# A fused attention and feed-forward kernel: the first batch in quarters of both weights, every engine in program order, and an ELU of relu and exp on ScalarE

## The chip, the cores and the metric

One core of a Trainium2 chip. The metric is the time of one execution in microseconds (us), measured on the device. The kernel before takes 883.1 us (median of 3 runs, 882.61 to 883.67). The experiments ran in rounds on four chips; the medians of the kernel before in them differ by 1.4 us, so differences of that size between experiments of different rounds can't be told from noise. In the profile PE is TensorE (matmuls), PEld its weight loads, DVE is VectorE, ACT is ScalarE, POOL is GpSimd, SP is SyncE; PEclk is the granted TensorE clock as a share of full speed. A float32 matmul shows as two records (passes) in these traces: the 544 matmuls of the second product are 1088 records in the page of the kernel before, and the 64 of a batch are 128. Where a line says x16, and where the text counts matmuls in a line of a trace, these are passes.

## The reference

Eight batches of eight heads. Each batch has 512 tokens and 32 state rows a head, of width 64. Tokens read the state and the state reads the tokens; the results go through a feed-forward layer with ELU. The weights arrive as float64.

```python
B, H, S, Ns, D = (8, 8, 512, 32, 64)
scores = scale * x @ state.T            # [512 x 32] a head
xread  = softmax(scores) @ state        # the tokens' result
scores2 = scale * state @ x.T           # [32 x 512] a head
sread  = softmax(scores2) @ x           # the states' result
x = concat([xread, sread], axis=2)      # -> (B * 544, 512)
h = x @ w_in                            # w_in  512 x 2048, float64
g = np.where(h > 0.0, h, np.exp(np.minimum(h, 0.0)) - 1.0)   # ELU
return g @ w_out                        # w_out 2048 x 512, float64
```

## The kernel before

The kernel never forms `xread`. For each quarter c of the hidden dimension it makes `m = state @ w_in` (the product of 32 state rows with 512 columns, per head), and then `h = a @ m`. A batch has 16 hidden tiles `fo` of 128 rows; the second product adds up 16 x 4 matmuls in four banks, as the text calls the 128x512 tiles of PSUM that the kernel's matmuls write. Where the text says that PE, DVE or ACT stands, that engine is idle, waiting for another. Float64 weights are made float32 in tiles of 128x512, 16 of `w_in` and 16 of `w_out`, by three instructions on ACT and four on DVE:

```python
def convert(dst, raw):
    words = raw.bitcast(U32).rearrange("p (j w) -> p j w", w=2)
    lo, hi = words[:, :, 0], words[:, :, 1]
    nc.scalar.activation(out=lo.bitcast(FP32), in_=lo, func=AF.Copy, scale=2.0**-29, bias=2.0**23)
    nc.scalar.activation(out=lo, in_=lo.bitcast(FP32), func=AF.Copy, bias=-(2.0**23))
    nc.scalar.activation(out=dst, in_=hi.bitcast(FP32), func=AF.Abs)
    nc.vector.tensor_scalar(out=dst, in0=dst, ...)            # clamp
    bits = dst.bitcast(U32)
    nc.vector.tensor_scalar(out=bits, in0=bits, ...)          # shift, mask
    nc.vector.scalar_tensor_tensor(out=bits, in0=hi, ...)     # sign
    nc.vector.tensor_tensor(out=bits, in0=bits, in1=lo, op=ALU.add)

def make_m(b, c):                       # m = state @ w_in, one quarter
    ...
    ps = by_state(b, "m_ps", [w_in[:, m, cols] for m in range(NP)])
    for g in range(G):
        (nc.scalar.copy, nc.vector.tensor_copy)[g % 2](out=m_t[b, c][:, g], in_=ps[:, g])

def elu(ps, g, fo):
    e = epool.tile([P, n], FP32, tag="e", name="e_sb")
    nc.scalar.activation(out=e, in_=ps, func=AF.Exp)
    nc.vector.tensor_scalar(out=e, in0=e, scalar1=1.0, scalar2=None, op0=ALU.min)
    nc.vector.scalar_tensor_tensor(out=g[fo], in0=e, scalar=-1.0, in1=ps, op0=ALU.add, op1=ALU.max)

...
for b in range(B):                      # batch 0 is the one with the weights
    g = {}
    for fo in range(FO):
        ffn1(g, b, fo)                  # h and ELU
        if b == 0:
            more(1)                     # one more conversion
        if fo % 4 == (3 if b == 0 else 1) and fo // 4 + 1 < FC:
            make_m(b, fo // 4 + 1)
    if b == 0:
        more(len(rest))                 # the 9 that are left, all of w_out
    hooks = attention(b + 1) if nxt else []
    ...                                 # second product, with the next
                                        # attention between its matmuls
```

Only PE keeps its written order here (`tc.keep_in_program_order` around each matmul and transpose). The instructions of ACT, DVE and POOL are placed by the scheduler when the program is built.

Of the kernel before, what the change touches and what calls it, by code (L numbers as in the profile page):

```python
# [25 lines left out]
def kernel(  # L26
# [23 lines left out]
    NB = S // 32  # L50
    scale = 1.0 / math.sqrt(D)
# [20 lines left out]
    rawpool = pool("raw", 7)  # L72
# [12 lines left out]
    def matmul(*args, **kw):  # L85
        tc.keep_in_program_order(nc.tensor.matmul(*args, **kw))  # L86

    def transpose(out, in_):
        tc.keep_in_program_order(nc.tensor.transpose(out, in_, ident))  # L89
# [22 lines left out]
    def load_states():  # L112
        s_v = state.rearrange("(q b) (m c) n d -> q c b n m d", q=2, c=2)
        raw = [
            rawpool.tile([P, NP, P], FP32, tag="raw", name="s_sb").rearrange(
                "p m (c d) -> p m c d", c=2
            )
            for q in range(2)
        ]
        for q in range(2):  # L120
            for b in range(B // 2):
                for c in range(2):
                    (nc.sync, nc.scalar)[q].dma_start(
                        out=raw[q][b * NS : (b + 1) * NS, :, c], in_=s_v[q, c, b]
                    )
        return raw

    def turn_states(raw):
        ps = banks([P, 2, NP, P], "k_ps")
        for q in range(2):  # L130
            for m in range(NP):
                transpose(ps[:, q, m], raw[q][:, m].rearrange("p c d -> p (c d)"))
        nc.vector.tensor_copy(
            out=kT.rearrange("p m (q s) -> p q m s", q=2), in_=ps
        )

    def load_weights(src):
        k = src.shape[-1]
        raw = rawpool.tile([P, 512], moe_w_in.dtype, tag="raw", name="raw")
        nc.sync.dma_start(out=raw.rearrange("p (j k) -> p j k", k=k), in_=src)  # L140
        return raw

    def convert(dst, raw):



        words = raw.bitcast(U32).rearrange("p (j w) -> p j w", w=2)
        lo, hi = words[:, :, 0], words[:, :, 1]

        nc.scalar.activation(  # L150
            out=lo.bitcast(FP32), in_=lo, func=AF.Copy, scale=2.0**-29, bias=2.0**23
        )
        nc.scalar.activation(out=lo, in_=lo.bitcast(FP32), func=AF.Copy, bias=-(2.0**23))


        nc.scalar.activation(out=dst, in_=hi.bitcast(FP32), func=AF.Abs)
        nc.vector.tensor_scalar(  # L157
            out=dst, in0=dst, scalar1=as_float(896 << 20),
            scalar2=as_float((1151 << 20) - 1), op0=ALU.max, op1=ALU.min,
        )  # L160

        bits = dst.bitcast(U32)
        nc.vector.tensor_scalar(  # L163
            out=bits, in0=bits, scalar1=3, scalar2=0x3FFFFFF8,
            op0=ALU.logical_shift_left, op1=ALU.bitwise_and,
        )
        nc.vector.scalar_tensor_tensor(  # L167
            out=bits, in0=hi, scalar=0xC0000000, in1=bits,
            op0=ALU.bitwise_and, op1=ALU.bitwise_or,
        )  # L170
        nc.vector.tensor_tensor(out=bits, in0=bits, in1=lo, op=ALU.add)  # L171
# [10 lines left out]
    def turn_x(b, i):  # L182

        ps = banks([P, 2, R, P], "xT_ps")
        for j in range(2):
            for r in range(R):
                m = 2 * i + j
                transpose(ps[:, j, r], x_t[b][:, r, m * P : (m + 1) * P])
        xT = xtpool.tile([P, 2, R * P], FP32, name="xT")
        for j in range(2):  # L190
            st[b, 2 * i + j] = xT[:, j]
            nc.scalar.copy(out=xT[:, j], in_=ps[:, j].rearrange("p r q -> p (r q)"))  # L192
# [18 lines left out]
    def scores(b):  # L211

        ps = by_state(b, "s_ps", [st[b, m] for m in range(NP)])
        for g in range(G):
            softmaxes(b, g, ps[:, g])

    def softmaxes(b, g, ps):

        top = small.tile([P, 1], FP32, name="top")
        total = small.tile([P, 1], FP32, name="total")  # L220
        nc.vector.reduce_max(top, ps, axis=AX_X)  # L221
        nc.vector.tensor_scalar(
# [3 lines left out]
        nc.vector.transpose(t.rearrange("p k n -> p (k n)"), ps)  # L226
        a = apool.tile([P, S], FP32, name="a_s")
        st[b, g, "a_s"] = a
        nc.scalar.activation(  # L229
            out=a, in_=ps, func=AF.Exp, scale=scale, bias=top, accum_out=total  # L230
        )

        top_t = small.tile([P, NB], FP32, name="top_t")
        total_t = small.tile([P, NB], FP32, name="total_t")
        nc.vector.reduce_max(top_t, t, axis=AX_X)  # L235
        nc.gpsimd.tensor_tensor(out=t, in0=t, in1=bc(top_t, NS), op=ALU.subtract)  # L236
        nc.scalar.activation(out=t, in_=t, func=AF.Exp, scale=scale)

        nc.vector.tensor_scalar(
            out=total, in0=total, scalar1=eps, scalar2=None, op0=ALU.add  # L240
        )
        nc.vector.reciprocal(out=total, in_=total)
        nc.vector.tensor_scalar(out=a, in0=a, scalar1=total, scalar2=None, op0=ALU.mult)

        nc.vector.reduce_sum(total_t, t, axis=AX_X)
        nc.vector.tensor_scalar(
            out=total_t, in0=total_t, scalar1=eps, scalar2=None, op0=ALU.add
        )
        nc.vector.reciprocal(out=total_t, in_=total_t)
        nc.gpsimd.tensor_tensor(out=t, in0=t, in1=bc(total_t, NS), op=ALU.mult)  # L250
        st[b, g, "t"] = t

    def turn_tokens(b, g):
        st[b, g, "aT"] = atpool.tile([P, S], FP32, name="aT")
        nc.vector.transpose(st[b, g, "aT"], st[b, g, "t"].rearrange("p k n -> p (k n)"))

    def turn_state(b):
# [6 lines left out]
        for g in range(G):  # L264
            nc.scalar.copy(out=st[b, "aT_s"][:, g], in_=ps[:, g])  # L265

    def state_read(b):
# [11 lines left out]
        for g in range(G):  # L279
            rows = slice(g * D, (g + 1) * D)  # L280
            nc.vector.tensor_copy(  # L281
# [3 lines left out]
    def make_m(b, c):  # L285
# [4 lines left out]
        for g in range(G):  # L290
            (nc.scalar.copy, nc.vector.tensor_copy)[g % 2](out=m_t[b, c][:, g], in_=ps[:, g])  # L291

    def elu(ps, g, fo):
# [3 lines left out]
        nc.scalar.activation(out=e, in_=ps, func=AF.Exp)  # L297
        nc.vector.tensor_scalar(out=e, in0=e, scalar1=1.0, scalar2=None, op0=ALU.min)  # L298
        g[fo] = gpool.tile([P, n], FP32, tag="g", name="g_sb")
        nc.vector.scalar_tensor_tensor(  # L300
# [3 lines left out]
    def ffn1(g, b, fo):  # L304
# [10 lines left out]
        elu(ps, g, fo)  # L315
# [14 lines left out]
    def ffn2(g, chunks, o_sb, hooks, every):  # L330

        ps = [ps_o.tile([P, DM], FP32, tag="o", name="o_ps") for c in chunks]
        done = 0
        for fo in range(FO):
            for c, o_ps in zip(chunks, ps):
                matmul(
                    o_ps,
# [8 lines left out]
        for c, o_ps in zip(chunks, ps):  # L346
            (nc.scalar.copy, nc.vector.tensor_copy)[c % 2](out=o_sb[c // 2][:, c % 2], in_=o_ps)  # L347

    def attention(b):

        nop = lambda: None
        steps = [lambda: turn_x(b, 0), lambda: turn_x(b, 1), lambda: scores(b), nop, nop]
# [3 lines left out]

    make_identity(nc, ident)
    raw_states = load_states()
    load_x(0, [nc.sync, nc.scalar])
    todo = [load_w_in(0, n) for n in range(NP)]  # L360
    turn_states(raw_states)
    steps = attention(0)
    for f in steps[:3]:
        f()
    for f in todo:
        f()
    todo = [load_w_in(1, n) for n in range(NP - 1)]
    make_m(0, 0)
    for f in steps[3:]:
        f()  # L370
    for f in todo:
        f()
    rest = [lambda c=c, n=n: load_w_in(c, n) for c in range(1, FC) for n in range(NP)][NP - 1 :]
    rest += [lambda fo=fo: load_w_out(fo) for fo in range(FO)]

    def more(k):
        for f in rest[:k]:
            f()()
        del rest[:k]

    for b in range(B):
        g = {}
        for fo in range(FO):
            ffn1(g, b, fo)
            if b == 0:
                more(1)
            if fo == 2 and b == 0:
                load_x(1, [nc.sync])
            if fo % 4 == (3 if b == 0 else 1) and fo // 4 + 1 < FC:
                make_m(b, fo // 4 + 1)  # L390
        if b == 0:
            more(len(rest))
        nxt = b + 1 < B
        hooks = attention(b + 1) if nxt else []
        if b + 2 < B:
            hooks += [lambda: load_x(b + 2, [nc.sync])]
        rows = out_b[b, 0:S].rearrange("(p r) c -> p r c", r=R)
        o_sb = [opool.tile([P, 2, DM], FP32, name="o_sb") for i in range(2)]
        for chunks in [[0, 1, 2], [3]] if b == 0 else [[0], [1], [2], [3]]:
            if nxt and chunks == [3]:  # L400
                hooks += [lambda: make_m(b + 1, 0)]
            ffn2(g, chunks, o_sb, hooks, 4)
            for i in range(2):
                if 2 * i + 1 in chunks:
                    nc.sync.dma_start(out=rows[:, 2 * i : 2 * i + 2], in_=o_sb[i])
# [3 lines left out]
    g = {}  # L409
    for fo in range(FO):  # L410
        ffn1_state(g, fo)
    o_sb = [opool.tile([P, 2, DM], FP32, name="o_sb")]
    for c in range(2):
        ffn2(g, [c], o_sb, [], 1)
        for i in range(P // NS):
            nc.sync.dma_start(
                out=out_b[c * (P // NS) + i, S:SB], in_=o_sb[0][i * NS : (i + 1) * NS, c]
            )
# [30 lines left out]
```

## Time and profile before

| | kernel before |
|---|---|
| time, median of 3 | 883.1 us |
| profiled run: span, mean clock | 882.8 us, 0.990 |
| PE busy | 838.0 us (95%) |
| DVE busy | 323.8 us, 658 instructions |
| ACT busy | 214.0 us, 386 instructions |
| batch 1's first product starts | 168.94 us |

PE is the bound from about 140 us on (busy for all 28.9 us from 140.0 to 168.9, and for 709.3 of the 713.9 behind them); the prediction shows the views for that. Here are the lines of PE's own timeline in batch 0 that have a wait, with the first h and the last line for their length (start, duration, what, count, and in brackets the idle time before with what ended it):

```profile
48.70 9.05 PE L86 MATMUL h_ps<-aT,m_sb 128*128 128x512 f32 x16
...
61.12 1.12 PE L86 MATMUL h_ps<-aT,m_sb 128*128 128x512 f32 x2 [2.36 <-ACT m_sb L291]
62.78 7.97 PE L86 MATMUL h_ps<-aT,m_sb 128*128 128x512 f32 x14 [0.54 <-DVE m_sb L291]
...
74.01 1.13 PE L86 MATMUL h_ps<-aT,m_sb 128*128 128x512 f32 x2 [2.24 <-ACT m_sb L291]
76.54 7.95 PE L86 MATMUL h_ps<-aT,m_sb 128*128 128x512 f32 x14 [1.41 <-DVE m_sb L291]
...
87.27 1.13 PE L86 MATMUL h_ps<-aT,m_sb 128*128 128x512 f32 x2 [1.76 <-ACT m_sb L291]
89.80 7.97 PE L86 MATMUL h_ps<-aT,m_sb 128*128 128x512 f32 x14 [1.40 <-DVE m_sb L291]
...
126.02 2.37 PE L89 MATMUL sT_ps<-ident,a_s 128*128 128x128 f32 x8 [4.68 <-ACT a_s L229]
128.18 5.07 PE L86 MATMUL o_ps<-w_out,g_sb 128*128 128x512 f32 x8
```

Between the first h at 48.70 and batch 1 at 168.94 PE stands still for 14.4 us in all (the sum of the brackets). Each group of 16 h matmuls takes about 9.1 us, though 8 of them take 3.43 at full clock (at 263.63, PEclk 1.00), so 16 should take 6.9: about 2.2 us a group are lost, 8.9 us in four groups, most of it to slow passes. In three of the groups PEclk shows them: 0.50 from 62.9 to 66.3, 0.51 from 76.5 to 80.0, 0.56 from 89.8 to 93.0. In the group at 48.70 it reads 1.00, but weight loads start 0.86 us apart until 52.2 and 0.43 from 52.9 on. The transposes at 126.02 lose 1.3 (1.04 at 101.04, PEclk 1.00), and the eight passes behind them 1.5 (5.07 for 3.60), at a clock of 0.50 from 126.0 to 131.0. So **everything that a better order of batch 0 can take out after 48.70 is about 14.4 + 8.9 + 1.3 + 1.5 = 26.1 us**.

### The profile page before, as it was taken

How to read it: one execution, taken by the hardware profiler on the slowest of the kernel's cores; microseconds unless marked ns; L12 is line 12 of the kernel's file. 1: busy time of each engine (PE TensorE's matmuls, PEld its weight loads, DVE VectorE, ACT ScalarE, POOL GpSimd, SP SyncE). 2: the span in 40 equal slices, each digit the busy share in tenths (PEclk: the TensorE clock that was granted, in tenths of full speed). 3: DMA queues.
4: the chain of work that ended last, by engine and by line, in shares of the span. 5: the costliest groups of instructions: out<-in, count | busy, mean ns of one | idle time of the engine just before them, and what ended most of it. 6: DMA issues, size and time to landing. Idle time of an engine off the chain costs nothing.

```text
span 882.8 us, 7236 instructions
## 1 busy us (share of the span) xinstructions
PE 838.0 (95%) x2824; PEld 391.5 (44%) x2824; DVE 323.8 (37%) x658; ACT 214.0 (24%) x386; POOL 35.8 (4%) x38
## 2 busy tenths in 40 slices
PE   3487979999999999999999999999999999999997
PEld 2242435444543454445444454445434544444763
DVE  2869980263105340444026301632053403500220
ACT  4757730132003210222013201321033102200110
POOL 0200010001000010001000100001000100000000
PEclk9999989999999999999999999999999999999999
DMA  8564502100300011000200030000000000000000
GB/s 256 149 177 155 184 9 48 48 1 1 71 1 25 0 36 36 25 0 1 72 24 1 1 71 25 0 1 25 0 25 0 1 25 24 1 0 25 24 1 24
DMA packets 42914, 35.07 MB, mean 40 GB/s; under 512 B 36480, under 2 KB 36480, under 8 KB 42880
## 3 DMA queue, kind: packets, MB, share of 16 engines
q1 hardware_dynamic: 39648, 33.82, 12.9%
q10 hardware_dynamic: 3232, 0.79, 0.4%
q8 instruction: 22, 0.36, 0.2%
q14 instruction: 12, 0.10, 0.0%
HBM read 25.69 MB, written 8.91 MB: 39 GB/s over the span
## 4 chain that ended last, share of the span: by engine, by line
PE 89%; DVE 6%; DMA 2%; ACT 2%; issue 1%; POOL 0%; SPq 0%; ACTq 0%
PE o_ps L86 51%; PE h_ps L86 28%; PE sr_ps L86 4%; PE m_ps L86 3%; PE xT_ps L89 1%; DMA raw<-in_moe_w_in_dram 1%; DVE w_out L167 1%; PE sT_ps L89 1%; PE s_ps L86 1%; DVE w_out L171 1%; DVE w_out L157 1%; DVE g_sb L300 0%; DVE w_out L163 0%; DVE w_in L167 0%; DMA x_sb<-in_x_dram 0%
## 5 line engine op out<-in xcount | busy, mean ns | idle before, releaser
L86 PE MATMUL o_ps<-w_out,g_sb 128*128 128x512 f32 x1088 | 478.6, 595 | 0.0
L86 PEld LDWEIGHTS o_ps<-w_out,g_sb 128*128 128x128 f32 x1088 | 204.1, 191 | 252.3 <-issue 249.3
L86 PE MATMUL h_ps<-aT,m_sb 128*128 128x512 f32 x512 | 235.3, 613 | 9.7 <-ACT m_sb L291 6.4
L86 PEld LDWEIGHTS h_ps<-aT,m_sb 128*128 128x128 f32 x512 | 97.6, 195 | 146.0 <-issue 105.0
L297 ACT ACTIVATE e_sb<-h_ps 128x512 f32<-128x512 f32 (+1 forms) x144 | 82.5, 573 | 247.7 <-PE h_ps L86 247.6
L298 DVE TENSOR_SCALAR e_sb<-e_sb 128x512 f32<-128x512 f32 (+1 forms) x144 | 59.3, 412 | 104.2 <-ACT e_sb L297 104.0
L300 DVE SCALAR_TENSOR_TENSOR g_sb<-e_sb,h_ps 128x512 f32<-128x512 f32 (+1 forms) x144 | 94.6, 657 | 4.5
L347 DVE COPY o_sb<-o_ps 128x512 f32<-128x512 f32 x17 | 11.7, 691 | 175.4 <-PE o_ps L86 175.4
L291 DVE COPY m_sb<-m_ps 128x512 f32<-128x512 f32 x32 | 22.1, 690 | 116.7 <-ACT m_sb L291 116.7
L347 ACT COPY o_sb<-o_ps 128x512 f32<-128x512 f32 x17 | 9.8, 579 | 216.0 <-PE o_ps L86 216.0
L86 PE MATMUL m_ps<-w_in,kT 64*32 64x512 f32 x512 | 39.5, 615 | 10.7 <-ACT a_s L229 7.4
L236 POOL TENSOR_TENSOR t_sb<-t_sb,top_t 128x512 f32<-128x512 f32 x16 | 16.9, 1059 | 645.0 <-DVE top_t L235 518.1
L221 DVE TENSOR_REDUCE top<-s_ps 128x1 f32<-128x512 f32 x16 | 11.0, 685 | 68.2 <-PE s_ps L86 68.2
L86 PEld LDWEIGHTS sr_ps<-aT_s,x_sb 128*128 128x128 f32 x256 | 33.0, 209 | 4.9 <-issue 3.3
L86 PE MATMUL sr_ps<-aT_s,x_sb 128*128 128x64 f32 x256 | 32.9, 292 | 1.2 <-ACT aT_s L265 1.2
L291 ACT COPY m_sb<-m_ps 128x512 f32<-128x512 f32 x32 | 18.7, 585 | 42.7 <-PE m_ps L86 42.7
L86 PE MATMUL h_ps<-xT_state,w_in 128*128 128x256 f32 x128 | 27.8, 379 | 0.0
L192 ACT COPY xT<-xT_ps 128x512 f32<-128x512 f32 x32 | 17.1, 588 | 43.6 <-PE xT_ps L89 43.6
L86 PEld LDWEIGHTS h_ps<-xT_state,w_in 128*128 128x128 f32 x128 | 24.3, 190 | 3.7 <-issue 0.5
L150 ACT ACTIVATE raw<-raw 128x512 f32<-128x512 uint32 x32 | 21.8, 680 | 12.9 <-DMA raw<-in_moe_w_in_dram 9.2
L86 PEld LDWEIGHTS m_ps<-w_in,kT 64*32 64x32 f32 x512 | 6.2, 105 | 39.4 <-issue 23.5
L281 DVE COPY xT_state<-sr_ps 64x128 f32<-64x128 f32 x16 | 4.6, 289 | 51.0 <-PE sr_ps L86 50.9
(42 smaller groups left out, 306.1 us busy)
## 6 DMA issues: line engine op xcount, KB each, us to landing
raw<-in_moe_w_in_dram SPq DMA_DIRECT2D x16, 512.0 KB, 5.0
raw<-in_moe_w_out_dram SPq DMA_DIRECT2D x16, 512.0 KB, 3.3
out_dram<-o_sb SPq DMA_DIRECT2D x16, 512.0 KB, 2.6
x_sb<-in_x_dram SPq DMA_DIRECT2D x30, 256.0 KB, 4.3
x_sb<-in_x_dram ACTq DMA_DIRECT2D x2, 256.0 KB, 4.7
out_dram<-o_sb SPq DMA_DIRECT2D x8, 64.0 KB, 1.7
s_sb<-in_state_dram SPq DMA_DIRECT2D x8, 32.0 KB, 2.1
s_sb<-in_state_dram ACTq DMA_DIRECT2D x8, 32.0 KB, 3.1
```

The costliest lines, as they stand in the source:

```text
L86: tc.keep_in_program_order(nc.tensor.matmul(*args, **kw))
L89: tc.keep_in_program_order(nc.tensor.transpose(out, in_, ident))
L150: nc.scalar.activation(out=lo.bitcast(FP32), in_=lo, func=AF.Copy, scale=2.0**-29, bias=2.0**23)
L157: nc.vector.tensor_scalar(out=dst, in0=dst, scalar1=as_float(896 << 20), scalar2=as_float((1151 << 20) - 1), op0=ALU.max, op1=ALU.min,)
L192: nc.scalar.copy(out=xT[:, j], in_=ps[:, j].rearrange("p r q -> p (r q)"))
L221: nc.vector.reduce_max(top, ps, axis=AX_X)
L236: nc.gpsimd.tensor_tensor(out=t, in0=t, in1=bc(top_t, NS), op=ALU.subtract)
L291: (nc.scalar.copy, nc.vector.tensor_copy)[g % 2](out=m_t[b, c][:, g], in_=ps[:, g])
L297: nc.scalar.activation(out=e, in_=ps, func=AF.Exp)
L298: nc.vector.tensor_scalar(out=e, in0=e, scalar1=1.0, scalar2=None, op0=ALU.min)
L300: nc.vector.scalar_tensor_tensor(out=g[fo], in0=e, scalar=-1.0, in1=ps, op0=ALU.add, op1=ALU.max)
L347: (nc.scalar.copy, nc.vector.tensor_copy)[c % 2](out=o_sb[c // 2][:, c % 2], in_=o_ps)
```

## The change

The intent: PE shall have second-product work while the weights still arrive. Batch 0 takes the weights in turn, a quarter of `w_in` and then a quarter of `w_out`, and its second product runs one quarter behind the first, in four banks at once. To make the order of batch 0 sure, ACT, DVE, POOL and SP keep program order there too, not PE alone. And the ELU uses `exp(-relu(-h))` for `min(exp(h), 1)`, two instructions on ACT and one on DVE in place of one and two.

```diff
+    class InOrder:
+        def __init__(self, engine):
+            self.engine, self.on = engine, True
+        def __getattr__(self, name):
+            def call(*args, **kw):
+                ins = getattr(self.engine, name)(*args, **kw)
+                return tc.keep_in_program_order(ins) if self.on else ins
+            return call
+    tensor, sync, vector, scalar, gpsimd = (
+        InOrder(e) for e in (nc.tensor, nc.sync, nc.vector, nc.scalar, nc.gpsimd)
+    )
 ...                                    (nc.vector -> vector and so on, throughout)
 def elu(ps, g, fo):
-        nc.scalar.activation(out=e, in_=ps, func=AF.Exp)
-        nc.vector.tensor_scalar(out=e, in0=e, scalar1=1.0, scalar2=None, op0=ALU.min)
+        scalar.activation(out=e, in_=ps, func=AF.Relu, scale=-1.0)
+        scalar.activation(out=e, in_=e, func=AF.Exp, scale=-1.0)
 ...                                    (softmax split in three parts)
+    def first_batch():
+        ...                             (loads, transposes of the states)
+        turn_x(0, 0)
+        turn_x(0, 1)
+        scores(0)
+        conv()                          # one tile of weights: convert, fetch another
+        for g in range(G):
+            softmax_2(0, g)
+        conv()
+        for g in range(G):
+            turn_tokens(0, g)
+        conv(2)
+        make_m(0, 0)
+        conv()
+        for g in range(G):
+            softmax_3(0, g)
+        turn_state(0)
+        g = {}
+        elus = [ffn1(g, 0, fo) for fo in range(2)]
+        state_read(0)
+        ...                             (four banks for the second product)
+        for c in range(FC):
+            for i in range(4):
+                if c == FC - 1 or i:
+                    conv()
+                elus.pop(0)()
+                if i < 2:
+                    elus.append(ffn1(g, 0, 4 * c + 2 + i))
+            if c > 0:
+                ffn2_part(g, chunks, o_ps, range(4 * c - 4, 4 * c))
+            if c + 1 < FC:
+                make_m(0, c + 1)
+                conv()
+                elus = [ffn1(g, 0, 4 * c + 4 + i) for i in range(2)]
+                conv(3)
+                if c + 2 < FC:
+                    conv()
+        for f in hooks[:3]:             # batch 1: transposes and scores
+            f()
+        ffn2_part(g, chunks, o_ps, range(FO - 4, FO))
+        for f in hooks[3:]:             # batch 1: state read
+            f()
+        make_m(1, 0)
+        ...                             (copies and stores of the result)
+    first_batch()
+    load_x(2, [sync])
+    for e in (vector, scalar, gpsimd):
+        e.on = False                    # later batches: free again
+    for b in range(1, B):
+        batch(b)
```

## The prediction

> **What bounds the kernel now.** I read the page first, then the ten-microsecond windows of the first 200 us, then the chain that ended last, and at the end the timeline of the first 170 us. The page's slices are 22 us wide:
>
> ```profile
> PE   3487979999999999999999999999999999999997
> DVE  2869980263105340444026301632053403500220
> ACT  4757730132003210222013201321033102200110
> ```
>
> From the seventh slice on PE is full; only the first six have holes. So the change, which is confined to batch 0 but for the ELU, can win or lose only there. The windows say what stands in its place:
>
> ```profile
> 20.00:30.00 10.00, 2.63 (x16) 0.20 (x8) 9.45 (x24) 9.84 (x20) 3.47 (x3) 1.00 0.87 211
> 80.00:90.00 10.00, 6.83 (x30) 2.39 (x29) 9.76 (x21) 7.62 (x14) 0.00 (x0) 1.00 0.43 137
> 110.00:120.00 10.00, 10.00 (x38) 4.20 (x23) 10.00 (x22) 3.76 (x7) 0.00 (x0) 1.00 0.09 34
> ```
>
> (Columns: PE, PEld, DVE, ACT, POOL busy, then clock, DMA share, GB/s.) While PE has holes DVE is nearly full: it turns float64 weights into float32, 32 tiles, the last at 121.0 in the timeline. Transfers have room. The chain gives the fixed points:
>
> ```profile
> 168.94 3.43 PE h_ps L86 x8
> ...
> 263.63 3.43 PE h_ps L86 x8
> ```
>
> Batch 1's first product starts at 168.94, batch 2's at 263.63: 94.7 us of unbroken PE work for each batch. Everything after 168.94 is 882.8 - 168.9 = 713.9 us of PE alone, and stays. The whole question is **when batch 1 starts**.
>
> [...]
>
> ```profile
> 50.51 0.34 PEld L86 LDWEIGHTS h_ps<-aT,m_sb 128*128 128x128 f32 x1 [0.52 <-issue]
> ...
> 53.29 0.19 PEld L86 LDWEIGHTS h_ps<-aT,m_sb 128*128 128x128 f32 x1 [0.24 <-issue]
> ```
>
> A pass costs 0.86 us cold and 0.43 warm, for about 4 us: each cold start loses some 2 us. [...]
>
> **The change part by part.** *ELU.* DVE loses the min, ACT gains a relu:
>
> ```profile
> L297 ACT ACTIVATE e_sb<-h_ps 128x512 f32<-128x512 f32 (+1 forms) x144 | 82.5, 573 | 247.7 <-PE h_ps L86 247.6
> L298 DVE TENSOR_SCALAR e_sb<-e_sb 128x512 f32<-128x512 f32 (+1 forms) x144 | 59.3, 412 | 104.2 <-ACT e_sb L297 104.0
> ```
>
> In batch 0 this takes 16 x 0.41 = 6.6 us from DVE and adds 16 x 0.57 = 9.2 us to ACT. Later both engines are under half busy beside a full PE: no effect.
>
> *The second product by quarters.* Before, its 64 matmuls (128 passes x 0.43 = 55 us) start at 97.6 and mostly trail the last conversion. Afterwards, only a quarter, 13.8 us, needs the last weights. If nothing else changed this would win some 25 us or more.
>
> *Program order.* The order of the built program shows its price, in three places. First, **a conversion is a chain** of four DVE instructions, each needing the one before. The first conversion of the kernel before stood alone:
>
> ```profile
> 16.77 0.43 DVE L157 TENSOR_SCALAR w_in<-w_in 128x512 f32<-128x512 f32 x1 [5.00 <-ACT w_in L156]
> 17.23 0.43 DVE L163 TENSOR_SCALAR w_in<-w_in 128x512 uint32<-128x512 uint32 x1
> 17.69 0.69 DVE L167 SCALAR_TENSOR_TENSOR w_in<-raw,w_in 128x512 uint32<-128x512 uint32 x1
> 18.42 0.69 DVE L171 CUSTOM_DVE_ANT_0 w_in<-raw,w_in 128x1024 uint16<-128x1024 uint16 x1
> ```
>
> Starts lie 0.46, 0.46, 0.73 apart; with 0.60 to the next independent instruction, 2.25 us. Where the scheduler wove two tiles together (from 113 us) the four spacings were 0.34, 0.34, 0.60, 0.60 = 1.88. So 32 x 0.37 = 12 us lost. ACT needs about 1.9 us a tile and leads.
>
> Second, ACT does batch 0's softmax before its first conversion. Third, and most: ACT's copy of each next m tile stands **before** the following conversions, and on PE that m product stands **behind** a quarter of the second product. So conversions wait while PE works, and then PE waits while they run: only two h banks turn over once the fourth output tile holds the third, so a quarter's last h tiles wait for ELUs that stand behind five conversions.
>
> I walk through it, times in us. kT copy ends at 11.8 as before; two rounds of transposes and copies, cold, then the scores end at 20.5. Both softmax halves in order (reductions 0.68, GpSimd 1.05, exps 0.65 each) keep ACT until 26.9. ACT's part of tile 0 takes 1.95: DVE converts from 28.9 (before: 16.8). With the sums and token transposes (1.13 twice, 0.6 twice) tiles 0 to 3 end at 41.5. Cold m0 1.9, copies, tile 4's ACT part: DVE resumes at 46, tile 4 at 48.3, scaling of a 1.7: 50.0. Then DVE's queue has the state-read copies: transposes 1.2 more, two h tiles cold 5.4, state read 3.5, so it stands until 60.1. Tiles 5 to 7 with four ELUs (0.66 each): 70. m1, copies, ACT lead: 73.9. Five tiles 11.3, ELU 4: 85.9. h7 cold 3.4, quarter 0 of the second product 13.8 plus some cold passes, then 103.4; m2 1.0, copy 0.6, ACT lead 2.0: **DVE resumes at 107.0**, idle since 94.5. Five tiles and ELU 8: 119. h10 and h11 (cold) to 124.5, quarter 1 to 138.3, m3, copy, lead: **141.9**, idle since 127.7. Four tiles 9.0, tile 28, ELU 12: 153.9; the last conversion ends at 161.9. On PE h14 and h15 end at 159.4, quarter 2 at 173.2, batch 1's transposes and scores with two copy waits 5.1: 178.3; quarter 3: 192.0; transposes, copy and state read 5.5, evacuation 0.6, m 1.0, two copies 1.4: **batch 1 starts at 200.5**.
>
> Sum on DVE: about 91 us of work from 28.9 would end at 120; five stands of 3.8, 10.1, 3.2, 11.8 and 13.6 add 42.5. Against 168.9 this is +31.6: 883.1 + 31.6 = **914.7 us**, 3.6% slower.
>
> **The rivals.**
> *A, overlap works as intended:* ACT and DVE run on without the stands, conversions end near 120, quarter 3 and the next attention (some 26) follow, batch 1 starts near 147: 861 us, 2.5% faster. For it: DVE was full and is relieved, PE's remainder shrinks from 55 to 14 us. Against it: the m copy really does stand ahead of the next conversions in ACT's queue, and its product really does stand behind 16 matmuls[...]. A wrong assignment of banks would only make two of the stands shorter.
> *B, a wash:* the cold starts vanish because the gaps are bridged by other work, the chained conversion overlaps better than the first one did, and the beginning loses 5 instead of 12 us: 20 us less, 895 us, within 2%. For it: several numbers come from a single instruction, and the beginning depends on when transfers land.
> *C, ACT becomes the bound:* it has about 32 x 1.9 + 16 x 1.2 + copies and softmax, some 94 us, as much as DVE. If a relu and an exp that reads its result cost more than 1.2 together, or a read of a fresh tile waits longer than 0.05, add 5 to 10: 920 to 925 us. The seven raw buffers cover about 16 us of conversions, so transfers shouldn't be a bound.
>
> **Range and chances.** The walk's weak terms are the cold passes (six times about 2 us, either way), the beginning (4 us either way) and the rate of conversion (0.15 us a tile, 5 us). They partly cancel: 902 to 928 holds it 8 times in 10. The 2% line is 900.8: slower 0.88, same 0.09, faster 0.03.
>
> **What would show it.** In the profile after: batch 1's first h product near 200, then 94.7 us a batch; DVE's first conversion near 29; an idle stand on DVE and ACT of 10 us or more ahead of the m copies near 105 and 140, released by PE's m product, with PE at the second product during it; PE idle near 80 to 86 and 109 to 119 while DVE converts, then at half rate; conversion starts 0.46, 0.46, 0.73 apart. If DVE converts without a break from 29 to 120, or if batch 1 starts before 169, the third step is wrong; if the two stands are there but the start is fast, only the first is. If later batches take longer than 94.7, the ELU was not free.

The sum came to 883.1 + 31.6 = 914.7 us. Two things stand in it as assumptions. One is that conversions wait behind an m copy that waits itself; in the kernel after ACT stands 13.03 us ahead of the copy at 104.49, and DVE 10.64 ahead of its own. The other is the 0.57 us for a relu, taken over from exp; the kernel after has 0.572 us for the relu and 0.606 for the exp behind it, and one table load, as before. The two weight-load lines give the two rates: 0.34 + 0.52 = 0.86 us a pass, which the trace of the kernel before has from about 48.7 to 52.9 (the "about 4 us"), and 0.19 + 0.24 = 0.43. In this document work is cold where its passes, or some of them, are spaced at about twice what the same work takes elsewhere, as 0.86 to 0.43, and else warm.

## The result

| | before | after |
|---|---|---|
| time, median | 883.38 us (882.61 to 884.90, 4 runs) | 920.44 us (916.94 to 922.94, 4 runs) |
| profiled run: time, mean clock | 884.56 us, 0.990 | 916.94 us, 0.981 |
| PE busy | 838.0 us | 839.9 us |
| DVE busy, instructions | 323.8 us, 658 | 278.7 us, 514 |
| ACT busy, instructions | 214.0 us, 386 | 300.3 us, 530 |
| batch 1 starts | 168.94 us | 201.05 us |

The time rose by 4.1%: the ratio is 1.0414, 95% interval 1.0377 to 1.0452. Ratios here are the mean time of one kernel's fast runs over that of the other's fast runs of the same rounds, so not quite the ratio of the medians quoted.

First the page's slices of the kernel after (22.9 us each):

```profile
PE   3376785889999999999999999999999999999997
DVE  1658457244320323032403240234023401400110
ACT  1448447226300631054104510352036202600230
```

PE has holes through the ninth slice, and DVE, which was nearly full from the second slice to the sixth but for the third, is now half empty beside them. Neither engine covers for the other. The windows tell how they alternate (columns: window; PE, PEld, DVE, ACT, POOL busy; clock, DMA share, GB/s):

```profile
20.00:30.00 10.00, 0.00 (x0) 0.00 (x0) 5.98 (x12) 6.51 (x13) 2.09 (x2) 1.00 0.02 7
90.00:100.00 10.00, 10.00 (x25) 4.46 (x24) 4.33 (x8) 1.43 (x3) 0.00 (x0) 1.00 0.40 141
110.00:120.00 10.00, 1.08 (x2) 0.57 (x3) 9.55 (x19) 9.81 (x18) 0.00 (x0) 0.66 0.72 208
130.00:140.00 10.00, 9.63 (x37) 3.66 (x35) 0.00 (x0) 0.27 (x1) 0.00 (x0) 1.00 0.09 34
```

From 110 to 120 DVE and ACT convert and PE is all but idle; from 130 to 140 PE multiplies and DVE and ACT do nothing. The DVE timeline has the stands, each with its releaser:

```profile
27.98 0.89 DVE L93 TENSOR_SCALAR w_in<-w_in 128x512 f32<-128x512 f32 x2 [3.59 <-ACT w_in L93]
...
60.24 0.59 DVE L93 COPY xT_state<-sr_ps 64x128 f32<-64x128 f32 x2 [10.38 <-PE sr_ps L93]
...
105.11 0.69 DVE L93 COPY m_sb<-m_ps 128x512 f32<-128x512 f32 x1 [10.64 <-ACT m_sb L93]
...
140.35 0.69 DVE L93 COPY m_sb<-m_ps 128x512 f32<-128x512 f32 x1 [11.57 <-ACT m_sb L93]
```

The two m copies name ACT's copy of the same bank as releaser, since that came last. ACT had itself been waiting, for PE; and PE was at the second product. These are PE's and ACT's lines around 103 to 105 and PE's next hole:

```profile
89.46 13.90 PE L93 MATMUL o_ps<-w_out,g_sb 128*128 128x512 f32 x32
103.29 1.09 PE L93 MATMUL m_ps<-w_in,kT 64*32 64x512 f32 x16
105.13 3.70 PE L93 MATMUL h_ps<-aT,m_sb 128*128 128x512 f32 x8 [0.75 <-ACT m_sb L93]
118.92 5.96 PE L93 MATMUL h_ps<-aT,m_sb 128*128 128x512 f32 x8 [10.09 <-DVE g_sb L93]
```

```profile
104.49 0.58 ACT L93 COPY m_sb<-m_ps 128x512 f32<-128x512 f32 x1 [13.03 <-PE m_ps L93]
```

So ACT stood 13.03 us for one m product of 1.09 us, which was queued behind a quarter of the second product. When it came, conversions resumed; PE then had two h tiles (the eight passes at 105.13), and the third needed a bank that an ELU had to clear, behind five conversions: a stand of 10.09, after which 8 h matmuls take 5.96 us in place of 3.70, since the clock had fallen (0.72 from 109.0 to 118.9, 0.50 from 118.9 to 122.0; 1.00 for the 3.70 at 105.13). The same pair returns at 139.7 and 154.2. In the chain of work that ended last, batches start at:

```profile
201.05 3.70 PE h_ps L93 x8
...
296.00 3.43 PE h_ps L93 x8
...
390.69 3.43 PE h_ps L93 x8
```

The later batches are as before: from 296.00 to 390.69 it is 94.69 us, as from 168.94 to 263.63 in the kernel before, for all that ACT now has 144 instructions more in the whole kernel.

### The profile page after: what moved, and what is told of

Its sections match the earlier page's. It is cut to its first block, busy times and chain, and to the rows that moved or that the text cites. A ratio compares the mean times of both kernels' runs of the same rounds, so it can differ in the third digit from the quotient of the medians.

```text
span 915.2 us, 7236 instructions
## 1 busy us (share of the span) xinstructions
PE 839.9 (92%) x2824; PEld 389.2 (43%) x2824; DVE 278.7 (30%) x514; ACT 300.3 (33%) x530; POOL 35.0 (4%) x38
## 4 chain that ended last, share of the span: by engine, by line
PE 89%; DVE 7%; ACT 2%; DMA 1%; issue 1%; POOL 0%; ACTq 0%
PE o_ps L93 51%; PE h_ps L93 27%; PE m_ps L93 4%; DVE w_out L93 3%; PE sr_ps L93 3%; DVE w_in L93 2%; PE xT_ps L93 2%; PE s_ps L93 1%; PE sT_ps L93 1%; DMA x_sb<-in_x_dram 1%; ACT raw L93 0%; ACT xT L93 0%; DMA s_sb<-in_state_dram 0%; DVE g_sb L93 0%; DVE total_t L93 0%
## 5 line engine op out<-in xcount | busy, mean ns | idle before, releaser
L93 PE MATMUL h_ps<-aT,m_sb 128*128 128x512 f32 x512 | 238.1, 618 | 29.7 <-DVE g_sb L93 26.8
L93 ACT ACTIVATE e_sb<-e_sb 128x512 f32<-128x512 f32 (+1 forms) x144 | 87.2, 606 | 4.5
L93 PE MATMUL m_ps<-w_in,kT 64*32 64x512 f32 x512 | 44.6, 619 | 20.6 <-ACT raw L93 10.8
L93 ACT ACTIVATE raw<-raw 128x512 f32<-128x512 uint32 x64 | 43.0, 672 | 1.0
L93 PEld LDWEIGHTS sr_ps<-aT_s,x_sb 128*128 128x128 f32 x256 | 29.8, 192 | 4.7 <-issue 3.1
L93 PE MATMUL sr_ps<-aT_s,x_sb 128*128 128x64 f32 x256 | 29.5, 274 | 1.2 <-ACT aT_s L93 1.2
L93 PE MATMUL xT_ps<-ident,x_sb 128*128 128x128 f32 x128 | 19.1, 294 | 5.0 <-ACT xT L93 2.3
```

What stands on the lines that cost most here:

```text
L93: ins = getattr(self.engine, name)(*args, **kw)
```

## The experiments

**Theory:** the loss is the program order on ACT and DVE. With it each of them stands behind a hand-over (m copy, state-read copy, ELU) that waits for another engine's long piece of work. **Rivals** (numbered, since the prediction has rivals A to C of its own): (1) the quarters lose by themselves, whatever the order; (2) the ELU with its second ACT instruction loads ACT, which leads every conversion; (3) cold clock after PE's stands is the larger part. Unless said otherwise an edit is to the kernel after. Percentages are against the kernel before in the same rounds (882.7 to 884.1 us).

### The ELU of before in the new order

```diff
-        scalar.activation(out=e, in_=ps, func=AF.Relu, scale=-1.0)
-        scalar.activation(out=e, in_=e, func=AF.Exp, scale=-1.0)
+        scalar.activation(out=e, in_=ps, func=AF.Exp)
+        vector.tensor_scalar(out=e, in0=e, scalar1=1.0, scalar2=None, op0=ALU.min)
```

> The changed kernel with the ELU of before put back (exp on ScalarE, min on VectorE). Queue theory (the loss is ScalarE and VectorE standing behind the m copies): VectorE gets 0.34 us back on each of about ten ELUs that lie on the path, so 3 us slower than the changed kernel, about 923 to 924 us. Rival, the relu and exp on ScalarE cost the time: at least 10 us faster, 910 us or less.

Measured 924.5 us (923.6 to 924.9), +4.6%. The new ELU is worth about 4 us here, so rival 2 falls: the ELU does not lose, it gains.

### The m product ahead of each quarter of the second product

```diff
+            if c + 1 < FC:
+                make_m(0, c + 1)
             if c > 0:
                 ffn2_part(g, chunks, o_ps, range(4 * c - 4, 4 * c))
             if c + 1 < FC:
-                make_m(0, c + 1)
                 conv()
```

> The changed kernel with each next m product put on TensorE ahead of the quarter of the second product instead of behind it, nothing else. Queue theory: the two stands of VectorE of about 11 us ahead of the m copies near 105 and 140 go, but the product then waits for the last w_in tile and the next ELU comes to stand behind the quarter, so a part of it comes back; batch 1 starts near 188 instead of 201, some 907 us. Rival, the stands are idle time that costs nothing because TensorE's own work is the bound there: same as the changed kernel, 920 us.

Measured 911.1 us (910.4 to 911.5), +3.1%: 9.3 us better than after where 13 were expected. Batch 1 starts at 193.48, not near 188. The stand is shortened, not gone: the waits up to batch 1 show ACT's m copy still at 29.3 us in total (longest 10.2; 47.0 and 13.0 in the kernel after), and ACT's waits for h tiles have risen from 10.3 us (longest 2.5) to 17.0 (longest 7.4). Right in direction, about two thirds in size.

### The beginning: conversions between the transposes and ahead of the softmax

```diff
         turn_x(0, 0)
+        conv()
         turn_x(0, 1)
-        scores(0)
         conv()
+        scores(0)
         for g in range(G):
             softmax_2(0, g)
         conv()
         for g in range(G):
             turn_tokens(0, g)
-        conv(2)
+        conv()
         make_m(0, 0)
```

> The changed kernel with the first two conversions put between the transposes and ahead of the softmax on ScalarE and VectorE, the rest as it is. Queue theory: the first m product ends near 37.8 instead of 43.5 and all that follows comes as much earlier: 5 to 6 us faster, about 915 us. Rival, the beginning is hidden behind the transfers: same, 920 us.

Measured 915.2 us (912.9 to 919.5), +3.6%: 5.3 better than after, as expected. The first h starts at 45.79, in the kernel after at 51.17. So about 5 of the 11 us by which the first conversion came late (27.98 for 16.77) could be had inside program order.

### The same program text with ACT, DVE and POOL free in batch 0

```diff
+    for e in (vector, scalar, gpsimd):
+        e.on = False
     first_batch()
     load_x(2, [sync])
-    for e in (vector, scalar, gpsimd):
-        e.on = False
```

> The changed kernel with program order kept on TensorE and SyncE alone; the scheduler orders ScalarE, VectorE and GpSimd in batch 0, as in the kernel before, but the work is in quarters. Queue theory: the first conversion comes near 17 instead of 28, conversions run ahead of the m copies and are woven in pairs, so most of the loss goes: 880 to 900 us. Rival, working in quarters is itself the loss (four output tiles open, two h banks left, TensorE cold after each wait): 912 us or more.

Measured **878.6 us** (875.7 to 879.0), -0.6% (ratio 0.9936, 0.991 to 0.9961). Taking away program order on three engines takes away 42 us, so the whole loss and a little more. Rival 1 falls. All three were freed at once; which of them has to be free was not tested. The DVE timeline and the waits of this kernel:

```profile
16.26 0.89 DVE L93 TENSOR_SCALAR w_in<-w_in 128x512 f32<-128x512 f32 x2 [4.73 <-ACT w_in L93]
```

```profile
ACT m_sb L93 <- PE m_ps L93: 15.0, 3, 8.2
...
DVE xT_state L93 <- PE sr_ps L93: 8.2, 2, 6.7
```

To be held against the kernel after in the same view (columns: us in total, times, longest):

```profile
ACT m_sb L93 <- PE m_ps L93: 47.0, 5, 13.0
...
PE h_ps L93 <- DVE g_sb L93: 26.8, 3, 10.1
...
DVE xT_state L93 <- PE sr_ps L93: 18.7, 2, 10.4
```

The wait of PE for ELUs, 26.8 us after, is 0.7 here.

But 878.6 is also the case where the change's real idea, the quarters, is alone with the ELU, and it is no faster than the old order with the new ELU (877.4, below; the ratios to the kernel before are 0.9936 and 0.9937). PE's timeline shows where it stands:

```profile
82.28 5.33 PE L93 MATMUL h_ps<-aT,m_sb 128*128 128x512 f32 x8 [3.66 <-ACT m_sb L93]
...
130.91 1.09 PE L93 MATMUL xT_ps<-ident,x_sb 128*128 128x128 f32 x8 [1.17 <-ACT xT L93]
133.17 1.84 PE L93 MATMUL s_ps<-xT,kT 64*32 64x512 f32 x16 [1.16 <-ACT xT L93]
...
151.88 5.31 PE L93 MATMUL sr_ps<-aT_s,x_sb 128*128 128x64 f32 x32 [1.16 <-ACT aT_s L93]
157.97 1.96 PE L93 MATMUL m_ps<-w_in,kT 64*32 64x512 f32 x16 [0.78 <-DVE xT_state L93]
160.66 5.39 PE L93 MATMUL h_ps<-aT,m_sb 128*128 128x512 f32 x8 [0.73 <-ACT m_sb L93]
```

PE keeps its written order, and in the new text batch 1's attention stands in two blocks, where the kernel before had its steps between the matmuls of the second product. Each step now waits for the copy of the last, 1.17 + 1.16 + 1.16 + 0.78 + 0.73 = 5.0 us, and some of the passes behind these waits are slow: the third line, for instance, takes 1.84 for what took 1.09 before. The granted clock is 0.91 from 120 to 140 and 0.85 from 140 to 160, and was 1.00 from 100 to 120. In all PE stands 11.8 us between its first h and batch 1 here; in the old order with the new ELU it is 11.0.

### Two tiles converted in turn, in program order

```diff
         def conv(k=1):
-            for i in range(k):
-                arriving.pop(0)()
-                fetch()
+            while k > 0:
+                two = [arriving.pop(0) for i in range(min(k, 2))]
+                convert_woven([t() for t in two])
+                for t in two:
+                    fetch()
+                k -= len(two)
 ...
+    def convert_woven(pairs):                    # ACT's three likewise, but Abs second
+        ...
+        for dst, lo, hi, bits in parts:
+            vector.tensor_scalar(...)            # clamp, one tile and then the other
+        for dst, lo, hi, bits in parts:
+            vector.tensor_scalar(...)            # shift, and so on
```

> The changed kernel with neighbouring conversions (14 of the 32 tiles, all of them in runs of two or more) woven in pairs in program order, each step for both tiles before the next step. Queue theory: each woven tile costs VectorE 1.88 us instead of 2.25, all on the path, 14 x 0.37 = 5 us faster: about 915 us. Rival, ScalarE or the transfers set the rate of conversion: same within 1 us, 920 us.

Measured 910.5 us (909.5 to 919.0), +3.3%. Three runs lie at 909.5 to 910.9 (clocks 0.983 to 0.985), and the profiled one at 919.0 (its clock 0.973). The gain is 10 us by the medians where 5 were expected; at like clocks it is 4 to 7 (919.0 against the kernel after's 922.94 at 0.973, the other three against its 916.94 at 0.981). And not all of it is weaving: the edit also puts ACT's Abs ahead of its second copy, so that DVE can begin sooner, and the seven waits of DVE for ACT's part of a tile fall from 10.4 us in sum to 7.1. The two were not tested apart. The chain of dependent instructions on DVE is a cost here (2.25 us a tile alone, 1.88 woven, in the kernel before), and by the walk's own sum (32 x 0.37 us) not the main one.

### TensorE kept warm through its stands

```diff
+        def keep_warm(n):                        # result is never read
+            ps = banks([P, G, 512], "warm_ps")
+            for k in range(n):
+                matmul(ps[:, k % G], kT[:, 0, 0:P], w_in[:, 0, 0:512], start=True, stop=True)
 ...
                 elus.pop(0)()
+                if c > 0 and i == (1 if c == 1 else 0):
+                    keep_warm(7 if c == 1 else 11)
```

> The changed kernel with idle matmuls, whose result nothing reads, in TensorE's three long pauses of batch 0 (7, 11 and 11 of them, 6 to 9.5 us) before h7, h10 and h14. Queue theory with cold starts: h7 falls from 3.65 to about 1.8 us, h10 and h11 together from 5.96 to about 3.5, h14 and h15 by about 1: 5 us faster, about 915 us, and the runs lie closer together. Rival, the matmuls after a pause are slow for another reason (banks, evacuation) or nothing depends on them: same or slower, 920 us or more.

Measured 918.5 us (916.0 to 918.9), +4.0%, mean clock 0.987 to 0.990. The h tiles behind the stands are now near the 1.88 us that four passes take in the finer order with free engines at a clock of 1.00 (80 to 100 us there):

```profile
85.13 1.98 PE L93 MATMUL h_ps<-aT,m_sb 128*128 128x512 f32 x4 [0.92 <-DVE g_sb L93]
```

The kernel after has for this tile 3.65 us, starting at 85.98. So the mechanism is as expected. But the time fell by 2 us, not 5. The profile of this run has its end of batch 0 cold: the state read at 192.01 takes 5.54 us, which the profiled run of the kernel after did in 3.79. So rival 3 is worth a few us, and no more.

### The kernel before with the new ELU alone

```diff
-        nc.scalar.activation(out=e, in_=ps, func=AF.Exp)
-        nc.vector.tensor_scalar(out=e, in0=e, scalar1=1.0, scalar2=None, op0=ALU.min)
+        nc.scalar.activation(out=e, in_=ps, func=AF.Relu, scale=-1.0)
+        nc.scalar.activation(out=e, in_=e, func=AF.Exp, scale=-1.0)
```

> The kernel before with only the new ELU (relu and exp on ScalarE, no min on VectorE). VectorE is near full until 121 us there, and loses 16 x 0.34 to 0.41 = 5 to 7 us of that, so the last conversion and the softmax of batch 1, for which TensorE waits 4.7 us near 126, come earlier: 3 to 5 us faster, 878 to 880 us. Rival, ScalarE delays its part of the conversions by as much: same, 883 us. The later batches, bound by TensorE, stay at 94.7 us in both.

Measured 877.4 us (876.3 to 878.1), -0.6% (0.9922 to 0.9952). The ELU part of the change gains about 5 us on its own. Batch 1 starts at 161.37, and its first product takes the usual 3.43 us.

### A finer order: tile by tile, still in program order

```diff
-        order = [lambda n=n: load_w_in(0, n) for n in range(NP)]
-        ...                                      # quarters in turn
+        w_ins = [lambda c=c, n=n: load_w_in(c, n) for c in range(FC) for n in range(NP)]
+        order = w_ins[:6]
+        for fo in range(FO):
+            order += w_ins[6 + fo : 7 + fo] + [lambda fo=fo: load_w_out(fo)]
 ...
+        for fo in range(FO):                     # woven in pairs, Abs second; two ahead of softmax
+            conv(2 if fo < 10 else 1)
+            elus.pop(0)()
+            if fo + 2 < FO:
+                elus.append(ffn1(g, 0, fo + 2))
+            if fo % 4 == 1 and fo // 4 + 1 < FC:
+                make_m(0, fo // 4 + 1)
+            if fo in extra:
+                extra[fo]()                      # state read; batch 1's attention
+            if fo > 0:
+                ffn2_part(g, chunks, o_ps, [fo - 1])
```

> The change's idea without its stands: all engines in program order, but the steps of one tile interleaved: for each h tile a pair of woven conversions (the next quarter's w_in and this tile's w_out), its ELU, the h product two tiles on, the second product of one tile before; m products a quarter ahead; first conversions before the softmax; the next attention's steps among the last six. Queue theory: for each tile TensorE has 5.4 us of work and VectorE about 4.7, so TensorE becomes the bound from about 39 us on, 98 us of work and a few of waits: batch 1 starts near 143, about 857 us, 3% faster than the kernel before. Rival, program order on all engines is bad however it is arranged (latencies of hand-over between engines add up): 880 us or more.

Measured 901.3 us (901.2 to 903.0), +2.1% (1.0198 to 1.0228): slower than the kernel before, and a miss of 44 us. The idea was that short pieces on every engine leave only short stands. The waits say otherwise:

```profile
ACT m_sb L93 <- PE m_ps L93: 40.0, 5, 17.0
...
PE h_ps L93 <- DVE g_sb L93: 28.9, 9, 9.6
...
DVE xT_state L93 <- PE sr_ps L93: 12.3, 2, 10.6
```

The same three hand-overs wait, for much the same sums. ACT, DVE and PE still stop for one another at each of them, now with one pair of tiles between; a hand-written order must fit all three queues at once, and this one did not.

### TensorE kept warm at the end of batch 0

```diff
-        for f in hooks[3:]:
-            f()
-        make_m(1, 0)
+        for f, n in zip(hooks[3:], [0, 0, 2, 1]):
+            f()
+            keep_warm(n)                         # here into a bank of the h pool
+        make_m(1, 0)
+        keep_warm(1)
```

> The changed kernel with four idle matmuls between the last quarter of batch 0's second product and batch 1's first product, where TensorE has three short waits and low work (two after the transposes of the state weights, one after the state read, one after the m product); they cost about 1 us beyond the waits. The profile of the changed kernel, its fastest run, had this stretch warm (state read 3.8, m 1.2, first h tiles 3.7 us); the profiles of four variants had it cold (5.1 to 5.7, 2.0, 5.2 to 6.7). Theory: the runs above the predicted time are those that go cold there; so the median falls to 915 to 917 us, and the profile shows state read near 3.6, m near 1.1, h tiles near 3.5. Rival, the higher times come from elsewhere: 920 us or more.

Measured 919.7 us (918.0 to 923.1), +4.2%: no gain, a miss of 3 us or more. In the profile the state read (3.68 us), the m product (1.09) and the first h (3.60 for eight passes) are warm, but the idle matmuls themselves stand in PE's queue (1.88 us for the first two, four passes), and the cold stretch is now elsewhere:

```profile
178.82 15.16 PE L93 MATMUL o_ps<-w_out,g_sb 128*128 128x512 f32 x32
```

The kernel after has 14.00 us for the same 32 matmuls, at 178.63. Which stretch is cold differs from profile to profile, so one can't say where the median loses.

### The finer order with ACT, DVE and POOL free

The edit is that of the finer order plus that of the free engines, both shown above.

> The finely interleaved kernel (901 us with all engines in program order) with program order kept on TensorE and SyncE alone. Queue theory: its loss came from copies and ELUs queued ahead of conversions on ScalarE and VectorE, so it falls below the quarters with a free scheduler (878.6) and below the kernel before with the new ELU (877.4): TensorE then has 98 us of work from about 41 us on, batch 1 starts at 143 to 150, 857 to 864 us. Rival, TensorE's fixed order is the limit (an h product waiting for an ELU holds the second product behind it): 875 us or more.

Measured **862.3 us** (860.55 to 862.88), -2.4% against the kernel before (ratio 0.9757, 0.974 to 0.9773), as expected: it beats both kernels. Batch 1 starts at 146.91, 22.0 us earlier than in the kernel before. In the chain:

```profile
37.92 6.66 PE h_ps L93 x8
...
146.91 3.43 PE h_ps L93 x8
```

In the kernel before the first of these lines is at 48.90, so 11.0 of the 22.0 us are won ahead of the first h, where the state read no longer stands (it now follows at 66.87), and 11.0 behind it. Its windows of 20 us from 60:

```profile
60.00:80.00 20.00, 20.00 (x77) 11.25 (x76) 16.61 (x35) 13.93 (x25) 0.00 (x0) 0.98 0.78 217
80.00:100.00 20.00, 20.00 (x62) 8.36 (x61) 20.00 (x43) 19.05 (x35) 0.00 (x0) 1.00 0.50 181
```

PE is full and warm (clock 0.98 and 1.00) while DVE and ACT convert beside it. This is what the change was after. How much of the gain is the weaving that the edit brings along was not tested.

### The quarters alone: free engines and the ELU of before

The edit is that of the first experiment plus that of the free engines.

> The quarters alone: the changed kernel with the scheduler free on ScalarE, VectorE and GpSimd, and with the ELU of before. With e4 (free, new ELU, 878.6), e7 (before with the new ELU, 877.4) and the kernel before this makes a square of ELU and quarters. If the parts add up, the quarters cost about 1 us and the ELU wins 5 to 6: about 884 us. Rival, the quarters win by themselves and the ELU took it away: 875 us or less.

Measured 881.6 us (878.4 to 881.8), -0.3% (0.9942 to 0.999). The quarters by themselves are worth about 2.5 us to the kernel before, where a loss of 1 was expected: the parts do not quite add up.

### Program order on the kernel before

The kernel before with the new ELU; ACT, DVE, POOL and SP keep program order until batch 1.

```diff
+    class InOrder: ...                           # as in the change
     for b in range(B):
+        if b == 1:
+            for e in (vector, scalar, gpsimd):
+                e.on = False
         g = {}
```

> The kernel before with the new ELU and program order on all engines in batch 0, but no quarters: the second product stays behind all of the first. Queue theory: the late first conversion (12 us), the chains (12 us) and the state-read copies (10 us) remain, while the m products no longer stand behind a quarter of the second product, so the stands of 11 us go; TensorE's 63 us after the first product hide a part: 895 to 908 us. Rivals: program order costs the same without quarters, 918 us or more; or it costs only together with the quarters, 877 to 882 us.

Measured 912.5 us (911.5 to 913.1), +3.3%, above the range I had expected. Program order alone costs 912.5 - 877.4 = 35 us without any quarters. The stands are others: every quarter's first ELU stands behind an m copy (3.46 us, three times), and the largest is new. Batch 1's copies of x on ACT are written behind all the remaining conversions, and PE's transposes wait for them in the middle of the second product:

```profile
118.16 3.60 PE L91 MATMUL o_ps<-w_out,g_sb 128*128 128x512 f32 x8
138.03 1.97 PE L91 MATMUL xT_ps<-ident,x_sb 128*128 128x128 f32 x8 [16.27 <-ACT xT L91]
```

### The parts side by side

Each cell is the ratio to the kernel before in the same rounds.

| | old ELU | new ELU |
|---|---|---|
| old order, three engines free | 1 (before) | 0.9937 |
| quarters, three engines free | 0.9966 | 0.9936 |
| old order, program order | not run | 1.0326 |
| quarters, program order | 1.0462 | 1.0414 (after) |
| tile by tile, program order | not run | 1.0213 |
| tile by tile, three engines free | not run | 0.9757 |

Down the right column: program order costs 3.9% on the old order, 4.8% on the quarters and 4.7% on the finer order. The ELU gains 0.3% to 0.6% in each row that has both.

## Why the prediction was right or wrong

**Time and direction: right.** Predicted 914.7 us, 902 to 928; measured 920.4. Batch 1 starts at 201.05 for a predicted 200.5.

**The third step, the stands: right.** The walk had 3.8, 10.1, 3.2, 11.8 and 13.6 us on DVE, 42.5 in sum. The trace has 3.7, 10.4, 3.2, 11.8 and 12.7 (the idle time of each stand, with the short wait for ACT's part of the next tile behind it for the four m stands), 41.8 in sum. Freeing the three engines took 42 us away, though that also frees the beginning and the chains, so the two numbers agree partly by chance. That the stands are caused by order is shown twice: by the free run, and by the m product put ahead, which shortened ACT's waits for m from 47.0 to 29.3 us and PE's for ELUs from 26.8 to 11.8, and gained 9.3 us.

**The first step, the chain: right in mechanism.** The kernel after converts every 2.25 us where conversions run on: in its DVE timeline conversions start at 109.18 and 111.43. In the kernel before a 0.43 us operation on DVE is followed by one that needs its result 0.46 us after its start, and by an independent one after 0.34; for a 0.69 us operation it is 0.73 and 0.60. Weaving 14 tiles in pairs gained 4 to 10 us, of which some 3 are DVE's shorter waits for ACT; that is in keeping with 14 x 0.37 = 5, but does not measure it. The sum of 12 was stated for all 32 tiles, which no experiment did alone.

**The second step, the start: right.** DVE's first conversion came at 27.98 for a predicted 28.9. Putting conversions ahead gained 5.3 us.

**The ELU later on: right.** Batches take 94.7 us as before. Its gain in batch 0 is 3 to 6 us, by three pairs of runs.

**Cold passes: mis-sized.** The median lies 5.7 us above the prediction, and this is not in the walk's stands: the profiled run, whose events match the walk to about a microsecond, took 916.94. The other three took 920.43, 920.46 and 922.94, at clocks of 0.975, 0.975 and 0.973 against 0.981. I had counted cold passes as "six times about 2 us, either way". They lie on one side: the profiled run was, by its clock, the one with the fewest. In the profiles of six experiments the last stretch ahead of batch 1 is cold where the kernel after's profile had it warm: its state read, m and first h take 4.1 us more in five of them and 5.8 in one. The four runs here differ by 0.65%; why a stretch is cold in one run and warm in another they don't show. Where exactly the median runs lose it stays open: only one of the four was traced, and keeping warm one place moved the time by 2 us, another by none. One reading of the prediction was wrong besides: it put the slow weight loads at 50.51 down to a pause, but PE had been at work without a break since 41.81. The two rates (0.86 and 0.43 a pass) are right. The state read ahead of them (32 passes with 64 columns) takes 7.09 us at 41.81 where it takes 3.68 at 133.09, so all of it ran at about half rate, and the h matmuls right behind it still lost about 2.2 us: over 7 us of PE work did not bring PE to the faster rate. (PEclk reads 1.00 there, so that column did not show this cold stretch.) Slow passes also came behind short stands: from 59.4 to 62.8 PE was busy for 1.14 of 3.40 us, its longest stand 2.36, and from 62.9 to 66.3 the clock was 0.50. What sets the rate was not shown.

**"If nothing else changed this would win some 25 us or more": wrong.** This is the step that failed, though the sum did not use it. The two quarters runs with free engines give 0.3% (2.5 us) with the old ELU and nothing with the new one (0.9936 against 0.9937). I had measured the gain by the length of the second product, 55 against 14 us. But PE in the kernel before was not waiting for weights in those 55 us; as its timeline shows, it stood still for 14.4 us in all after 48.70 and lost about 12 in slow passes, 26.1 together. So 25 was not the gain but nearly all there was to gain, and to get it PE must have no hole at all. The quarters closed some holes and opened others, at each m copy and in batch 1's attention steps, which no longer stood between matmuls: 11.8 us of stands against 11.0. The finer order with free engines came nearest: 22.0 us earlier at batch 1, half of it because its first h starts at 37.92.

The prediction's **rival A** (861 us) described what the change could have been, and the finer order with free engines reaches it, at 862.3, though by another order of work than the one rival A was reckoned for. Its argument against itself, that the m copy and its product stand where they do, holds for the written order (ACT stood 13.03 us for one m product), not for the scheduler's. **Rival B** (895) is rejected: there was no 20 us in overlap, and the clock erred to the other side. **Rival C** (920 to 925) names the time that came, but not for its reason: a relu and an exp behind it took 0.57 and 0.61 us in the kernel after, about the 1.2 assumed, and the new ELU gained.

## What to carry to other kernels

A program order that is fixed on all engines has to fit every queue at once; where one queue's hand-over stood here behind another's long piece of work, both engines stopped in turn (ACT for 13.03 us and then PE for 10.09). In none of the three orders written here did it fit: fixing it cost 35, 42 and 39 us. Before putting a gain on a rearrangement, add up the idle and cold time of the engine that bounds the end: that sum, not the length of the work that is moved, is the most that can be won in that stretch (here 26.1 us behind the first h). Then write the fine order for the one engine that must have it, and try the others with the scheduler free: here that won each time.
